# Loading batch 0 ahead, batch 1's transposes on TensorE, and pv per head with a column of ones

## The chip, the cores and the metric

The kernel runs on one core of a Trainium2 chip. The metric is the device time of one execution in microseconds (us). A profiled execution is read beside the timed ones; its times are us from the first instruction of the program. The engines are named as in the profile: PE is TensorE's matmuls and PEld its weight loads, DVE is VectorE, ACT is ScalarE, POOL is GpSimd, SP the queue that issues the DMAs.

## The reference

Sliding-window attention over 8 batches of 576 tokens with 8 heads of 64, and then a token mixer and an MLP on the result. Heads 0 to 3 see the last 32 tokens, heads 4 to 7 every fourth of the last 128.

```python
scores = scale * q @ k.T                      # (8, 8, 576, 576), scale 1/8
mask_plain = (rel >= 0) & (rel < 32)          # heads 0..3
mask_dil = (rel >= 0) & (rel < 128) & (rel % 4 == 0)   # heads 4..7
attn = exp(scores - max) ; attn /= sum(attn) + 1e-9
x = concat_heads(attn @ v)                    # (8, 576, 512), float32
h = x.T @ U @ V                               # U (576, 32), V (32, 576)
u = x + h.T
out = u + relu(u @ w_ch1) @ w_ch2             # 512 -> 2048 -> 512
```

The weights U, V, w_ch1 and w_ch2 reach the chip as 64-bit numbers and are turned into pairs of 32-bit numbers there.

## The kernel before, in words

**Attention.** The tokens of the dilated heads are reordered, so that both kinds of head have a band of 32. A batch has 9 blocks of 64 queries for each kind. A unit is one pair of heads and one block: its two heads lie in the 128 partitions of a tile (query of head 0, then of head 1), and its keys are 96. Four units are a group, 9 groups a batch (`NGB`). For a group, `score` multiplies queries and keys on TensorE (L392 in batches 0 and 1, L381 in most later groups, which are twice as wide and split into high and low parts first), `soften` masks and takes the negated maximum on DVE (L412) and the exponential on ACT (L416), whose accumulator gives the sum of the exponentials. `turn` transposes the result: on TensorE with a copy by DVE (L429, L433) for groups below `PE_T` = 12, that is batch 0 and three groups of batch 1, and otherwise with eight 32-row transposes on DVE (L442, L445). `weighted` multiplies by the values, four matmuls of 128 by 96 by 128, one for each unit (L453). One unit's product holds both heads' rows against both heads' values, of which only the two diagonal blocks are used. Each fp32 matmul appears as two instructions of TensorE. Then DVE adds 1e-9 to the sums (L454), takes the reciprocal (L455) and writes the products into the token tiles (L481); the dilated half goes through `xp` and DMAs (L485). A group's steps are spread over three turns of a loop (`LAG` = 2).

**Mixer and MLP.** For each batch, `split` makes high and low parts of x (L499, L501), `t_mm` multiplies by U (L521), `t_evict` and `mix` by V and add (L530 to L547). Token tiles are transposed (`transp`, L576 to L582, or `turn_x`) and go in chunks of three tiles through the MLP: 16 slices `f` of the hidden layer, for each 12 matmuls `ph` (L748), ReLU and split into `hh` on ACT and `hl` on DVE (L753, L754), and 9 matmuls `acc` (L765). The MLP is the bulk of TensorE's work. `weight_step` converts the weights piece by piece on ACT, DVE and POOL (L209 to L225).

**Order.** Batch 0's attention and mixer run first, then the MLP of the first chunk begins; the steps of batches 1 to 7 wait in a list, `queue`, with due times, and are put between the matmuls of the chunks. Weights are converted during batch 0, at a lower priority, and in the first chunk. A scheduler orders each engine's instructions at build time by priority and expected readiness. All loads go through SP.

**Loads of batches 0 and 1.** `load_qk` and `load_v` load a whole group, 448 KB of queries and keys and 192 KB of values. Five of the first and four of the second are issued ahead of all else (`FETCH` = 5); each turn of the loop issues those of a later group. Groups below `NE` = 7 take their queries and keys from such tiles, in four buffers (`QKS`); groups 7 and 8, and batch 1, fetch pairs of units (`fetch`, L339) into three buffers (`TB`). The pool `early` holds what batch 0 alone needs and is closed when it ends.

Of the kernel before, what the change touches and what calls it, by code (L numbers as in the profile page):

```python
# [10 lines left out]
F32 = mybir.dt.float32  # L11
F32R = mybir.dt.float32r
BF16 = mybir.dt.bfloat16
# [5 lines left out]
ALU = mybir.AluOpType  # L19

B, H, S, D = 8, 8, 576, 64
# [5 lines left out]
P = 128  # L27
QB = 64
NJ = S // QB
KB = QB + WIN  # L30
# [9 lines left out]
NCHUNK = NTILE // CT  # L40
UNITS = 4
QK1 = P + KB
KW = P + WIN
QK2 = P + KW
QK3 = P + 2 * KW
# [2 lines left out]
NGB = len(TILES) // 2  # L48
# [3 lines left out]
LAG = 2  # L52
# [7 lines left out]
H_ON_ACT = 3  # L60
XL_DVE = ((0, 1), (1, 1))
AHEAD = 2
FETCH = 5
POST_AT = 0.7
TAIL = 0.25
BLK = P // WIN
ZS = 2
NE = 7
QKB = 3
AHEAD_AT = 0.9  # L70
LO0 = 0.1
TB = 3
# [14 lines left out]
F_LAST = 13  # L87
RAWS = 4
VS = 4
QKS = 4  # L90
XPS = 4
VBS = 7
DVE_FROM = 2
TURN_AT = 0.5
TURN_GAP = 0.08
PT_ACT = ()
PE_T = 12
MASK_AT = (None, -16, 0, 16, 32, 48)
WIDE_AT = (None, 0, 16, 32, 48)
NEG = -8.0e9  # L100
# [50 lines left out]
def attention_moe_kernel(ctx: ExitStack, tc: tile.TileContext, qk1, qk2, vv, masks, wide, ident, ut, vt, w1, w2, out):  # L151
# [22 lines left out]
    HM = len(MASK_AT) // 2  # L174
    mask_sb = [work.tile([P, HM, KB], F32, tag="qk", name=f"mask{i}", bufs=QKB) for i in range(2)]
    spare = work.tile([P, QK2], F32, tag="qk", name="spare", bufs=QKB)
    wide_sb = const.tile([P, len(WIDE_AT), KW], BF16, name="wide_sb")
    id_sb = const.tile([P, P], F32, name="id_sb")
    us = const.tile([P, 9, 2 * RANK], F32R, name="us")
    vs = const.tile([P, P + S], F32R, name="vs")  # L180
# [117 lines left out]
    loaded = {}  # L298

    def load_qk(g):  # L300
        if g >= NE:
            if g == NE:
                for i in range(0, 2 * TB, 2):
                    fetch(UNITS * g + i)
        elif (g, 0) not in loaded:
            t = early.tile([P, UNITS, QK1], F32, tag="qk", name=f"qk{g}", bufs=QKS)
            nc.sync.dma_start(out=t, in_=qk1[g])
            loaded[g, 0] = t

    def load_v(g, i):  # L310
        if (g, 1, i) not in loaded:
            us_ = slice(2 * i, 2 * i + 2)
            if g < NGB:
                if i == 0:
                    t = early.tile([KB, UNITS, P], F32, tag="v", name=f"v{g}", bufs=VBS)
                    nc.sync.dma_start(out=t, in_=vv[g])
                    loaded[g, 1, 0] = t[:, 0:2]
                    loaded[g, 1, 1] = t[:, 2:4]
            else:
                t = work.tile([KB, 2, P], F32, tag="v", name=f"v{g}_{i}", bufs=3)  # L320
                nc.sync.dma_start(out=t, in_=vv[g][:, us_])
                loaded[g, 1, i] = t

# [44 lines left out]
    def score(g, u):  # L368
        n = UNITS * g + u
        two = n >= N2 and not is_odd(n)  # L370
        if u == 0:
            p_sb = work.tile([P, UNITS, KW], F32, tag="p", name=f"p{g}", bufs=2)
            pool, n_ = (early, 3) if g < NGB else (work, 2)
            nmax = pool.tile([P, UNITS], F32, tag="nmax", name=f"nmax{g}", bufs=n_)
            ssum = pool.tile([P, UNITS], F32, tag="ssum", name=f"ssum{g}", bufs=n_)
            state[g] = [p_sb, nmax, ssum, None]
        if two:
            sp = psum.tile([P, 2 * KW], F32, tag="ps", name=f"s{g}_{u}")
            split_qk(n)
            t = pairs.pop(n)  # L380
            nc.tensor.matmul(sp, lhsT=t[:, 0:P], rhs=t[:, P:], start=True, stop=True)  # L381
        else:
            if n >= N2:
                sp = psum.tile([P, 1, KB], F32, tag="ps", name=f"s{g}_{u}")
            elif u == 0:
                sp = psum.tile([P, UNITS, KB], F32, tag="acc" if g < NGB else "ps", name=f"s{g}", bufs=3)
            else:
                sp = state[g][3]
            if g >= NE:
                fetch(n)  # L390
            t = raws[n] if g >= NE else loaded[g, 0][:, u]
            nc.tensor.matmul(sp[:, u % sp.shape[1], :], lhsT=t[:, 0:P], rhs=t[:, P:QK1], start=True, stop=True)  # L392
        state[g][3] = state[g, u] = sp

    def soften(g, u):
        n = UNITS * g + u
        p_sb, nmax, ssum, _ = state[g]
        sp = state.pop((g, u))
        half, j = tile_of(g, u)
        every = slice(0, P)  # L400
        if n < N2:
            kind = mask_kind(half, j)
            todo = [(every, KB, sp[:, u], mask_sb[kind // HM][:, kind % HM])]
        elif is_odd(n):
            todo = [(slice(QB * h, QB * (h + 1)), KB, sp[QB * h:QB * (h + 1), 0],
                     wide_sb[QB * h:QB * (h + 1), 0, QB * h:QB * h + KB]) for h in range(2)]
        else:
            kind = mask_kind(half, tile_of(g, 0)[1] // 2, WIDE_AT, P)
            nc.vector.tensor_tensor(out=p_sb[:, u, :], in0=sp[:, 0:KW], in1=wide_sb[:, kind], op=ALU.add)  # L409
            todo = [(every, KW, sp[:, KW:], p_sb[:, u])]  # L410
        for rs, w, a, c in todo:
            nc.vector.tensor_tensor_reduce(  # L412
                out=p_sb[rs, u, 0:w], in0=a, in1=c, scale=-1.0 / 8.0, scalar=3.0e38,
                op0=ALU.add, op1=ALU.min, accum_out=nmax[rs, u:u + 1],
            )
        nc.scalar.activation(  # L416
            out=p_sb[:, u, 0:w], in_=p_sb[:, u, 0:w], func=AF.Exp,
            bias=nmax[:, u:u + 1], scale=-1.0, accum_out=ssum[:, u:u + 1],
        )

    def is_wide(g):
        return g >= SPLIT * NGB and g % NGB != ODD
# [22 lines left out]
                    nc.vector.transpose(out=pt[ks, :, rs], in_=p_sb[rs, :, ks])  # L445
        return pt

    def weighted(g, pt, ssum):
        b = g // NGB
        pv = psum.tile([P, UNITS, P], F32, tag="ps", name=f"pv{g}")  # L450
        for u in range(UNITS):
            v_sb = loaded[g, 1, u // 2]
            nc.tensor.matmul(pv[:, u, :], lhsT=pt[:, u, :], rhs=v_sb[:, u % 2, :], start=True, stop=True)  # L453
        nc.vector.tensor_scalar(out=ssum, in0=ssum, scalar1=1e-9, scalar2=None, op0=ALU.add)  # L454
        nc.vector.reciprocal(out=ssum, in_=ssum)  # L455
        moves = []
        xp = None
        for i in range(2):
# [18 lines left out]
            dst4 = dst.rearrange("p (u h d) -> p u h d", u=2, h=2)  # L477
            for h in range(2):
                rs = slice(QB * h, QB * (h + 1))
                norm = ssum[QB * i:QB * (i + 1), h::2] if is_wide(g) else ssum[rs, us_]  # L480
                nc.vector.tensor_tensor(  # L481
                    out=dst4[:, :, h, :], in0=pv[rs, us_, h * D:(h + 1) * D],
                    in1=norm.unsqueeze(2).broadcast_to([QB, 2, D]), op=ALU.mult)
        for t, to, n, r in sorted(moves):
            nc.sync.dma_start(out=x_tile(t)[to:to + DIL * (n - 1) + 1:DIL, HALF_D:], in_=xp[r:r + n])  # L485
        if moves and b == 0:
# [97 lines left out]
    def batch_items(b):  # L584
# [3 lines left out]
        for s in range(NGB + LAG):  # L588
            g = NGB * b + s

            def pre(s=s, g=g):
                if b == 0:
                    for i in (g, g + 1, g + FETCH):
                        if i < NGB:
                            load_qk(i)
                    if g + FETCH - 1 < NGB:
                        load_v(g + FETCH - 1, 0)
                if 0 < s <= NGB:
                    load_v(g - 1, 0)
                if s >= LAG:  # L600
                    weighted(g - LAG, *held.pop(g - LAG))
                if b > 0 and 0 < s <= NGB:
                    load_v(g - 1, 1)

            def post(s=s, g=g):
                late = g - (NGB * b < PE_T)
                if late in state and late not in turned:
                    turned.add(late)
                    p_sb, _, ssum, _ = state.pop(late)
                    held[late] = (turn(late, p_sb), ssum)  # L610

            def some(us, g=g):
                for u in us:
# [60 lines left out]
    early_open = ExitStack()  # L674
    early = early_open.enter_context(tc.tile_pool(name="early", bufs=1))
    held_u.append(early.tile([P, len(DPART), 2 * RANK], F32R, name="us_d"))
    for g in range(FETCH):
        load_qk(g)
        if g == 0:
            for i in range(2):  # L680
                nc.sync.dma_start(out=mask_sb[i], in_=masks[:, HM * i:HM * (i + 1)])
        if g == 1:
            nc.sync.dma_start(out=id_sb, in_=ident)
        if g < FETCH - 1:
            load_v(g, 0)
    pre = batch_items(0)
    w_prio = [tc.cur_priority + W_OFF]
    for i, (_, it) in enumerate(pre):
# [11 lines left out]
    for _ in range(PRE_N):  # L700
        weight_step(NSMALL, NPIECE)
    tc.cur_priority = now
    early_open.close()
    make_w(F_MID, F_LAST, None)

    def ahead(stage):
# [87 lines left out]
def lay_out(q, k, v, U, V, w1, w2):  # L794
# [1 line left out]
    f = np.float32  # L796
    qk1 = np.zeros((B, len(TILES), 2, P, QK1), f)
    qk2 = np.zeros((B - SPLIT, NGB, UNITS, P, QK2), f)
    vv = np.zeros((B, len(TILES), 2, KB, P), f)
    for half in range(2):  # L800
        perm = np.array([token_of(half, s) for s in range(S)])
        hs = slice(half * HH, (half + 1) * HH)
# [5 lines left out]
        for j in range(NJ):  # L808
            at = TILES.index((half, j))
            ks = slice(QB * j, QB * j + KB)  # L810
            for h in range(2):
                hr = slice(h * D, (h + 1) * D)
                qk1[:, at, :, hr, h * QB:(h + 1) * QB] = qp[:, :, h, QB * j:QB * (j + 1)].transpose(0, 1, 3, 2)
                qk1[:, at, :, hr, P:] = kp[:, :, h, ks].transpose(0, 1, 3, 2)
                vv[:, at, :, :, hr] = vp[:, :, h, ks]
        for i in range(NJ // 2):
            g = TILES.index((half, 2 * i)) // 2
            for u in range(UNITS):
# [4 lines left out]
    qk2[:, ODD, :, :, :QK1] = qk1[SPLIT:, ODD]  # L823
    qk2 = qk2.reshape((B - SPLIT) * NGB * UNITS, P, QK2)
    qk1 = np.ascontiguousarray(qk1[:SPLIT].reshape(SPLIT * NGB, UNITS, P, QK1).transpose(0, 2, 1, 3))
    vv = np.ascontiguousarray(vv.reshape(B * NGB, UNITS, KB, P).transpose(0, 2, 1, 3))

    masks = np.stack([np.tile(mask_of(off, QB), (2, 1)) for off in MASK_AT], axis=1)
    wide = np.stack([mask_of(off, P) for off in WIDE_AT], axis=1).astype(ml_dtypes.bfloat16)
# [41 lines left out]
```

## Time and profile before

| | |
|---|---|
| median of 3 runs | 1032.8 us (1031.57 to 1034.27) |
| profiled execution | 1032.92 us, span 1031.1 us |
| mean granted TensorE clock | 0.974 |
| PE, busy | 992.3 us (96%) |
| PEld, busy | 894.4 us (87%) |
| DVE, busy | 643.8 us (62%) |
| ACT, busy | 436.8 us (42%) |
| POOL, busy | 323.4 us (31%) |
| bytes moved | 103.05 MB |

The page of the profile gives each engine's busy time, the span in 40 slices of 25.8 us with the busy tenths of each, the chain of work that ended last, and groups of equal instructions with their count, busy time and mean length. The matmuls of TensorE overlap in their pipeline, so a matmul's own length is more than what it holds up; what it holds up is read from one start to the next.

### The profile page before, as it was taken

The page shows a single profiled execution, that of the slowest core. Times are in us where ns is not written, and L with a number is a line of the kernel's source. Part 1 is how long each engine was busy: PE and PEld are TensorE (multiplying, and loading weights), DVE is VectorE, ACT ScalarE, POOL GpSimd, SP SyncE. Part 2 cuts the span into 40 slices and gives each one's busy share as a digit, 9 for nine tenths or more (in the row PEclk, how much of TensorE's full clock was granted, in tenths as well). Part 3 has the DMA queues.
Part 4 walks back from the last instruction along what each step waited for, and adds up shares of the span by engine and source line. Part 5 has one row for each costly group of instructions (what it writes and reads, how often), then busy time and mean ns, then how long its engine had stood idle before and what let it go on. Part 6 is the DMA issues. An engine that isn't in the chain of part 4 may idle for free.

```text
span 1031.1 us, 17355 instructions
## 1 busy us (share of the span) xinstructions
PE 992.3 (96%) x5304; PEld 894.4 (87%) x5304; DVE 643.8 (62%) x2197; ACT 436.8 (42%) x1274; POOL 323.4 (31%) x519
## 2 busy tenths in 40 slices
PE   6769998999999999999999999999999999999998
PEld 5658887998899899998899898999889898999996
DVE  5888987877457863877557864777647874311211
ACT  5888874454244432444233532544324442111110
POOL 1476644353132630434122621335213431000000
PEclk9658999999999999999999999999999999999999
DMA  9767544243232433333232432424223321400000
GB/s 281 215 197 231 173 142 118 78 128 87 78 98 71 123 84 78 108 104 99 72 96 80 128 82 61 131 82 126 85 73 86 119 65 30 125 1 1 31 1 31
DMA packets 97197, 103.05 MB, mean 100 GB/s; under 512 B 12848, under 2 KB 84080, under 8 KB 97104
## 3 DMA queue, kind: packets, MB, share of 16 engines
q1 hardware_dynamic: 97104, 101.94, 34.6%
q8 instruction: 43, 0.70, 0.3%
q14 instruction: 50, 0.41, 0.1%
HBM read 79.86 MB, written 17.30 MB: 94 GB/s over the span
## 4 chain that ended last, share of the span: by engine, by line
PE 82%; DVE 10%; DMA 4%; ACT 3%; issue 1%; SPq 0%; POOL 0%; DVEq 0%; POOLq 0%; ACTq 0%
PE ph L748 36%; PE acc L765 35%; PE pv L453 5%; PE s L381 3%; PE t L521 2%; DVE pt L445 2%; DMA qk<-qk 1%; PE s L392 1%; DVE utl L582 1%; DMA qkr<-qk 1%; DMA v<-vv 1%; DVE v L217 1%; PE m L545 1%; ACT p L416 1%; DVE xp L481 1%
## 5 line engine op out<-in xcount | busy, mean ns | idle before, releaser
L765 PE MATMUL acc<-w2h,hh 128*128 128x512 f32 x576 | 229.4, 398 | 0.0
L765 PE MATMUL acc<-w2l,hh 128*128 128x512 f32 x576 | 228.5, 397 | 0.0
L357 POOL TENSOR_TENSOR qks<-qkr,qks 128x160 fp32r<-128x160 f32 x192 | 104.5, 544 | 376.8 <-ACT qks L356 254.4
L765 PE MATMUL acc<-w2h,hl 128*128 128x512 f32 x576 | 213.4, 397 | 1.6 <-DVE hl L754 1.6
L753 ACT ACTIVATE hh<-ph 128x384 fp32r<-128x384 f32 x192 | 93.6, 487 | 284.4 <-PE ph L748 274.6
L754 DVE SCALAR_TENSOR_TENSOR hl<-ph,hh 128x384 fp32r<-128x384 f32 x192 | 106.0, 552 | 167.5 <-ACT hh L753 167.0
L416 ACT ACTIVATE p<-p,nmax 128x160 f32<-128x160 f32 (+1 forms) x288 | 117.2, 408 | 137.4 <-DVE nmax L412 135.3
L748 PE MATMUL ph<-uth,w1h 128*128 128x384 f32 x768 | 175.3, 342 | 0.0
L748 PE MATMUL ph<-uth,w1l 128*128 128x384 f32 x768 | 174.6, 340 | 0.0
L748 PE MATMUL ph<-utl,w1h 128*128 128x384 f32 x768 | 173.3, 339 | 0.0
L748 PEld LDWEIGHTS ph<-uth,w1h 128*128 128x128 f32 x768 | 139.5, 190 | 15.0 <-ACT uth L581 0.3
L748 PEld LDWEIGHTS ph<-uth,w1l 128*128 128x128 f32 x768 | 136.8, 189 | 0.5
L748 PEld LDWEIGHTS ph<-utl,w1h 128*128 128x128 f32 x768 | 135.8, 188 | 1.5
L765 PEld LDWEIGHTS acc<-w2h,hl 128*128 128x128 f32 x576 | 108.1, 189 | 24.4 <-DVE hl L754 2.5
L442 DVE STREAM_TRANSPOSE pt<-p 32x128 f32<-32x128 f32 x384 | 115.9, 302 | 19.7 <-ACT p L416 14.5
L765 PEld LDWEIGHTS acc<-w2h,hh 128*128 128x128 f32 x576 | 109.2, 190 | 15.6 <-ACT hh L753 0.2
L765 PEld LDWEIGHTS acc<-w2l,hh 128*128 128x128 f32 x576 | 109.1, 189 | 14.8
L356 ACT CAST qks<-qkr 128x288 fp32r<-128x288 f32 x192 | 81.7, 430 | 84.7 <-PE s L381 58.7
L360 POOL TENSOR_TENSOR qks<-qkr,qks 64x128 fp32r<-64x128 f32 x192 | 90.1, 470 | 15.1
L409 DVE TENSOR_TENSOR p<-s,wide_sb 128x160 f32<-128x160 f32 x192 | 60.6, 319 | 46.6 <-PE s L381 44.6
L453 PE MATMUL pv<-v,pt 96*128 96x128 f32 x576 | 80.1, 283 | 3.8 <-DVE pt L445 1.7
L453 PEld LDWEIGHTS pv<-v,pt 96*128 96x128 f32 x576 | 77.2, 199 | 7.1 <-DVE pt L433 2.0
(68 smaller groups left out, 1052.9 us busy)
## 6 DMA issues: line engine op xcount, KB each, us to landing
qkr<-qk SPq DMA_DIRECT2D x192, 144.0 KB, 2.2
raw<-w SPq DMA_DIRECT2D x26, 512.0 KB, 5.1
v<-vv SPq DMA_DIRECT2D x126, 96.0 KB, 2.1
out<-x SPq DMA_DIRECT2D x36, 256.0 KB, 2.3
zd<-z SPq DMA_DIRECT2D x120, 64.0 KB, 1.9
xt<-zd SPq DMA_DIRECT2D x30, 256.0 KB, 2.8
qkr<-qk SPq DMA_DIRECT2D x22, 224.0 KB, 3.4
qk<-qk SPq DMA_DIRECT2D x7, 448.0 KB, 7.7
```

The lines of the kernel that those rows point to most:

```text
L356: nc.scalar.copy(out=t[:, 0:QK2], in_=raw)
L357: nc.gpsimd.tensor_tensor(out=t[:, QK2:], in0=raw[:, P:], in1=t[:, P:QK2].bitcast(F32), op=ALU.subtract)
L360: eng.tensor_tensor(out=t[lo, 0:P], in0=raw[lo, 0:P], in1=t[lo, 0:P].bitcast(F32), op=ALU.subtract)
L381: nc.tensor.matmul(sp, lhsT=t[:, 0:P], rhs=t[:, P:], start=True, stop=True)
L409: nc.vector.tensor_tensor(out=p_sb[:, u, :], in0=sp[:, 0:KW], in1=wide_sb[:, kind], op=ALU.add)
L416: nc.scalar.activation(out=p_sb[:, u, 0:w], in_=p_sb[:, u, 0:w], func=AF.Exp, bias=nmax[:, u:u + 1], scale=-1.0, accum_out=ssum[:, u:u + 1],)
L442: nc.vector.transpose(out=to[:, :, WIN * (r % 2):WIN * (r % 2 + 1)], in_=p_sb[rs, :, QB * s + WIN * k:QB * s + WIN * (k + 1)])
L453: nc.tensor.matmul(pv[:, u, :], lhsT=pt[:, u, :], rhs=v_sb[:, u % 2, :], start=True, stop=True)
L748: nc.tensor.matmul(ph, lhsT=w[:, k, :], rhs=u[:, k, :], start=(n == 0), stop=(n == len(seq) - 1))
L753: nc.scalar.activation(out=hh, in_=ph, func=AF.Relu)
L754: nc.vector.scalar_tensor_tensor(out=hl, in0=ph, scalar=0.0, in1=hh.bitcast(F32), op0=ALU.max, op1=ALU.subtract)
L765: nc.tensor.matmul(acc[i], lhsT=h[:, ss], rhs=w, start=(f == 0 and n == 0), stop=(f == FC - 1 and n == 2))
```

## The change

Three things are changed together.

1. All nine groups of batch 0 are loaded whole, each into its own buffer (`NE` and `QKS` are 9), and all these loads are issued at the start, the second half of the masks after the third group. The values go into slots of the pool of the x tiles. The first three fetches of batch 1 stand behind batch 0's steps. The wide masks get a place in a pool that opens when `early` closes.
2. `PE_T` becomes 18: groups 12 to 17, the last six of batch 1, are transposed on TensorE.
3. `weighted` multiplies each head by itself: eight matmuls for a group, with 64 columns of the transposed exponentials as weights and 65 columns of values, the last of which is one. Head 0's product goes to partitions 0 to 63 and head 1's to 64 to 127. The 65th column is the sum, which DVE reads from PSUM; the exponential on ACT has no accumulator any more. The loaded values have 65 columns for each head.

```diff
+DV = D + 1
+PV = 2 * DV
-FETCH = 5
-NE = 7
+NE = 9
-QKS = 4
+QKS = 9
-VBS = 7
-PE_T = 12
+PE_T = 18
...
     def load_qk(g):
-        if g >= NE:
-            if g == NE:
-                for i in range(0, 2 * TB, 2):
-                    fetch(UNITS * g + i)
-        elif (g, 0) not in loaded:
+        if (g, 0) not in loaded:
             t = early.tile([P, UNITS, QK1], F32, tag="qk", name=f"qk{g}", bufs=QKS)
...
-                    t = early.tile([KB, UNITS, P], F32, tag="v", name=f"v{g}", bufs=VBS)
+                    t = xpool.tile([P, UNITS, PV], F32, tag="x", name=f"v{g}")[0:KB]
...
-                t = work.tile([KB, 2, P], F32, tag="v", name=f"v{g}_{i}", bufs=3)
+                t = work.tile([KB, 2, PV], F32, tag="v", name=f"v{g}_{i}", bufs=3)
...
         nc.scalar.activation(
             out=p_sb[:, u, 0:w], in_=p_sb[:, u, 0:w], func=AF.Exp,
-            bias=nmax[:, u:u + 1], scale=-1.0, accum_out=ssum[:, u:u + 1],
+            bias=nmax[:, u:u + 1], scale=-1.0,
         )
...
-    def weighted(g, pt, ssum):
+    def weighted(g, pt):
         b = g // NGB
-        pv = psum.tile([P, UNITS, P], F32, tag="ps", name=f"pv{g}")
+        pv = psum.tile([P, UNITS, DV], F32, tag="ps", name=f"pv{g}")
         for u in range(UNITS):
             v_sb = loaded[g, 1, u // 2]
-            nc.tensor.matmul(pv[:, u, :], lhsT=pt[:, u, :], rhs=v_sb[:, u % 2, :], start=True, stop=True)
-        nc.vector.tensor_scalar(out=ssum, in0=ssum, scalar1=1e-9, scalar2=None, op0=ALU.add)
+            for h in range(2):
+                hs = slice(h * DV, (h + 1) * DV)
+                nc.tensor.matmul(pv[QB * h:QB * (h + 1), u, :], lhsT=pt[:, u, QB * h:QB * (h + 1)],
+                                 rhs=v_sb[:, u % 2, hs], start=True, stop=True)
+        pool, n_ = (early, 3) if g < NGB else (work, 2)
+        ssum = pool.tile([P, UNITS], F32, tag="ssum", name=f"ssum{g}", bufs=n_)
+        nc.vector.tensor_scalar(out=ssum, in0=pv[:, :, D], scalar1=1e-9, scalar2=None, op0=ALU.add)
         nc.vector.reciprocal(out=ssum, in_=ssum)
...
-                norm = ssum[QB * i:QB * (i + 1), h::2] if is_wide(g) else ssum[rs, us_]
                 nc.vector.tensor_tensor(
-                    out=dst4[:, :, h, :], in0=pv[rs, us_, h * D:(h + 1) * D],
-                    in1=norm.unsqueeze(2).broadcast_to([QB, 2, D]), op=ALU.mult)
+                    out=dst4[:, :, h, :], in0=pv[rs, us_, 0:D],
+                    in1=ssum[rs, us_].unsqueeze(2).broadcast_to([QB, 2, D]), op=ALU.mult)
...
             def pre(s=s, g=g):
-                if b == 0:
-                    for i in (g, g + 1, g + FETCH):
-                        if i < NGB:
-                            load_qk(i)
-                    if g + FETCH - 1 < NGB:
-                        load_v(g + FETCH - 1, 0)
...
-    for g in range(FETCH):
+    for g in range(NGB):
         load_qk(g)
         if g == 0:
-            for i in range(2):
-                nc.sync.dma_start(out=mask_sb[i], in_=masks[:, HM * i:HM * (i + 1)])
-        if g == 1:
+            nc.sync.dma_start(out=mask_sb[0], in_=masks[:, 0:HM])
             nc.sync.dma_start(out=id_sb, in_=ident)
-        if g < FETCH - 1:
-            load_v(g, 0)
+        if g == 2:
+            nc.sync.dma_start(out=mask_sb[1], in_=masks[:, HM:])
+        load_v(g, 0)
...
+    for i in range(0, 2 * TB, 2):
+        fetch(UNITS * NGB + i)
     early_open.close()
+    rest = ctx.enter_context(tc.tile_pool(name="rest", bufs=1))
+    wide_sb = rest.tile([P, len(WIDE_AT), KW], BF16, name="wide_sb")
     make_w(F_MID, F_LAST, None)
...
-    vv = np.zeros((B, len(TILES), 2, KB, P), f)
+    vv = np.ones((B, len(TILES), 2, KB, PV), f)
...
-                vv[:, at, :, :, hr] = vp[:, :, h, ks]
+                vv[:, at, :, :, h * DV:h * DV + D] = vp[:, :, h, ks]
```

More of the change, by code (lines that the diff above doesn't have):

```diff
@@ L176, in attention_moe_kernel @@
     spare = work.tile([P, QK2], F32, tag="qk", name="spare", bufs=QKB)
-    wide_sb = const.tile([P, len(WIDE_AT), KW], BF16, name="wide_sb")
     id_sb = const.tile([P, P], F32, name="id_sb")
@@ L374, in score @@
             nmax = pool.tile([P, UNITS], F32, tag="nmax", name=f"nmax{g}", bufs=n_)
-            ssum = pool.tile([P, UNITS], F32, tag="ssum", name=f"ssum{g}", bufs=n_)
-            state[g] = [p_sb, nmax, ssum, None]
+            state[g] = [p_sb, nmax, None]
         if two:
@@ L387, in score @@
             else:
-                sp = state[g][3]
+                sp = state[g][2]
             if g >= NE:
@@ L392, in score @@
             nc.tensor.matmul(sp[:, u % sp.shape[1], :], lhsT=t[:, 0:P], rhs=t[:, P:QK1], start=True, stop=True)
-        state[g][3] = state[g, u] = sp
+        state[g][2] = state[g, u] = sp
     def soften(g, u):
         n = UNITS * g + u
-        p_sb, nmax, ssum, _ = state[g]
+        p_sb, nmax, _ = state[g]
         sp = state.pop((g, u))
@@ L600, in pre @@
                 if s >= LAG:
-                    weighted(g - LAG, *held.pop(g - LAG))
+                    weighted(g - LAG, held.pop(g - LAG))
                 if b > 0 and 0 < s <= NGB:
@@ L608, in post @@
                     turned.add(late)
-                    p_sb, _, ssum, _ = state.pop(late)
-                    held[late] = (turn(late, p_sb), ssum)
+                    held[late] = turn(late, state.pop(late)[0])
             def some(us, g=g):
@@ L825, in lay_out @@
     qk1 = np.ascontiguousarray(qk1[:SPLIT].reshape(SPLIT * NGB, UNITS, P, QK1).transpose(0, 2, 1, 3))
-    vv = np.ascontiguousarray(vv.reshape(B * NGB, UNITS, KB, P).transpose(0, 2, 1, 3))
+    vv = np.ascontiguousarray(vv.reshape(B * NGB, UNITS, KB, PV).transpose(0, 2, 1, 3))
     masks = np.stack([np.tile(mask_of(off, QB), (2, 1)) for off in MASK_AT], axis=1)
```

## The prediction

> **What bounds the kernel now.** I read the page first: the engines' shares, the 40 slices and the chain.
>
> ```profile
> span 1031.1 us, 17355 instructions
> PE 992.3 (96%) x5304; PEld 894.4 (87%) x5304; DVE 643.8 (62%) x2197; ACT 436.8 (42%) x1274; POOL 323.4 (31%) x519
> PE   6769998999999999999999999999999999999998
> DVE  5888987877457863877557864777647874311211
> ACT  5888874454244432444233532544324442111110
> PEclk9658999999999999999999999999999999999999
> PE 82%; DVE 10%; DMA 4%; ACT 3%; issue 1%; SPq 0%; POOL 0%; DVEq 0%; POOLq 0%; ACTq 0%
> ```
>
> TensorE is full from the seventh slice on. Only the first six, some 155 us, are not all its own: there DVE and ACT mostly stand at 8, and the granted clock falls to 0.5 in one slice. So two prices are wanted: what the change does to TensorE's own time, which is paid in full after about 180 us, and what it does to the stretch before. The windows put sizes to it.
>
> ```profile
> 0.00:26.00 26.00, 16.59 (x101) 14.84 (x101) 13.69 (x80) 13.33 (x54) 3.26 (x8) 0.98 0.97 281
> 26.00:70.00 44.00, 29.85 (x124) 24.00 (x125) 39.79 (x99) 36.48 (x90) 26.36 (x23) 0.58 0.68 210
> 70.00:180.00 110.00, 101.48 (x552) 89.81 (x551) 89.30 (x274) 83.21 (x225) 64.92 (x61) 0.94 0.55 167
> 180.00:1031.00 851.00, 844.39 (x4532) 765.72 (x4530) 501.05 (x1747) 303.82 (x908) 228.81 (x428) 1.00 0.29 80
> ```
>
> The columns are TensorE, its weight loads, DVE, ACT, POOL, granted clock, DMA share and GB/s. Up to 26 us the DMA is the limit (0.97 of the time) and DVE has 12.3 us idle. From 26 to 70 DVE works 39.8 of 44 us and ACT 36.5. After 180 us no engine but TensorE is near its limit. The profiled execution took 1032.9 us in all, 1.8 more than its span and 0.1 more than the median of the three runs; the sum is made against it. About 0.3% (3.1 us) is what a measurement of this kernel can tell from no change.
>
> **The loads first.** Batch 0 needs nine query/key and nine value tiles. Today seven of the query/key tiles come through four buffers, and the last two groups in pairs through three others. These rows, of the timeline and of the groups, show what that makes late and what DVE spends on a group.
>
> ```profile
> 27.79 2.77 PE L392 MATMUL s<-qkr 128*128 128x96 f32 x12
> ...
> 36.86 0.69 PE L392 MATMUL s<-qkr 128*128 128x96 f32 x4
> ...
> 28.88 2.03 SPq L339 DMA_DIRECT2D qkr<-qk  x3
> ...
> 49.49 1.22 DVE L481 TENSOR_TENSOR xp<-pv,ssum 64x128 f32<-64x128 f32 x4
> ```
>
> ```profile
> L412 DVE CUSTOM_DVE_ANT_0 p<-s,mask 128x96 f32<-128x96 f32 x72 | 14.3, 252 | 12.2 <-PE s L392 12.0
> L433 DVE COPY pt<-ptp 96x512 f32<-96x512 f32 x12 | 8.2, 682 | 3.0 <-PE ptp L429 2.7
> ```
>
> The pair for the last scores of batch 0 is issued at 28.9 us, the scores run at 36.9, and the last weighting on DVE ends at 50.7. After the change the queue holds 9 x 448 KB, 9 x 195 KB, the masks and the identity, 6.1 MB, ahead of anything else; at the 281 GB/s of the first window that has landed by about 24 us. A group costs DVE four softmax steps (0.2 each), a copy (0.69), four weightings (1.22) and two small operations on the sums: some 3 us, 27 for nine. If DVE starts at 6 us and works four fifths of the time, 16 of these are done by 26; with 7 us that I allow for splits and small weights the rest ends at about 44 instead of 50.7. Against these 6 to 7 us stands that U, V and the MoE weights now queue on SP behind six more loads, and ACT has to convert them.
>
> ```profile
> 19.06 0.62 ACT L209 ACTIVATE v<-raw 128x448 f32<-128x448 f32 x1 [0.75 <-DMA raw<-ut]
> ...
> 32.50 0.68 ACT L209 ACTIVATE v<-raw 128x512 f32<-128x512 f32 x1 [2.15 <-DMA raw<-w]
> ```
>
> The first of these moves from 19 to some 25 us, and with it about 4.5 us of ACT work into the stretch where ACT is short. The second stands behind 7.8 MB, 28 us at that rate, so it need not be later than its 32.5. I take -6 us. The ends are -12, all of DVE's idle time in the first window, and +3, ACT's 4.5 us with little gained elsewhere. Batch 1's first pairs, today the other two issues of the row at 28.9 us, are written behind batch 0's steps and are wanted only once the MoE runs. The wide masks, loaded after batch 0's pool closes, are read from batch 2 on; batch 1 covers both, and without that cover TensorE would stand for a load's time, once. The value tiles take nine slots of the x pool beside batch 0's five, of 16, so none waits.
>
> **The sums.** ACT loses a read of its accumulator.
>
> ```profile
> L416 ACT ACTIVATION_READ_ACCUMULATOR p<-p,nmax 128x1 f32 x288 | 54.4, 189 | 0.0
> ...
> 23.06 0.35 ACT L416 ACTIVATE p<-p,nmax 128x96 f32<-128x96 f32 x1
> 23.32 0.19 ACT L416 ACTIVATION_READ_ACCUMULATOR p<-p,nmax 128x1 f32 x1
> 23.41 0.36 ACT L416 ACTIVATE p<-p,nmax 128x96 f32<-128x96 f32 x1
> ```
>
> Start to start a step takes 0.35 us; without the read the next could start at 23.32, 0.09 earlier. That is 26 us over 288 steps: worth nothing after 180 us, where ACT works 304 of 851 us, and 3.2 us in each of the first two batches. The first 3.2 are spent against the 4.5 above; for batch 1 I take -1.5 (ends 0 and -3.2). On DVE the small sum (L454) now reads PSUM and has to follow the matmul. The weightings behind it waited for the same matmul already, so what is queued behind them on DVE, the `hl` that TensorE needs in the MoE, is held by the two small operations at most, 0.35 us a group; DVE's idle third after 180 us covers it, and without that cover 54 groups would pay 19 us.
>
> **Batch 1's transposes.** Between 69 and 180 us DVE's groups have these rows:
>
> ```profile
> L445 DVE STREAM_TRANSPOSE pt<-p 32x128 f32<-32x128 f32 x48 | 14.5, 301 | 1.7 <-ACT p L416 1.1
> ...
> L454 DVE TENSOR_SCALAR ssum<-ssum 128x4 f32<-128x4 f32 x9 | 6.2, 690 | 0.2
> ```
>
> and TensorE's timeline these:
>
> ```profile
> 110.39 1.05 PE L453 MATMUL pv<-v,pt 96*128 96x128 f32 x8
> 111.28 1.03 PE L392 MATMUL s<-qkr 128*128 128x96 f32 x8
> ...
> 118.92 1.16 PE L453 MATMUL pv<-v,pt 96*128 96x128 f32 x8 [1.71 <-DVE pt L445]
> ...
> 121.79 0.63 PE L765 MATMUL acc<-w2h,hl 128*128 128x512 f32 x1
> 122.22 0.63 PE L765 MATMUL acc<-w2h,hh 128*128 128x512 f32 x1
> ```
>
> The 48 transposes are the six groups that move, 14.5 us, against six copies, 4.1: DVE gets 10 back. TensorE takes on 24 instructions of 128 columns; at the 111 ns that the eight of `pv` take each (0.89 us to the next start) that is +2.6, and since TensorE works 92% of this stretch I charge all of it. It buys off one stall, 1.7 us, and behind it eight matmuls at the slow clock, 0.43 us apart where 0.23 is usual: 3.3 in all. Net -0.7; the ends are +2.6, the stall merely changing its cause, and -6, if the other waits of the stretch shrink too. ACT, 83 of 110 us busy, is late next. L454's 690 ns for four numbers a row is mostly not work; whether a PSUM source avoids it no row shows, and as it is DVE's time I count none of its 4 us.
>
> **The weighting per head, on TensorE.** Instead of eight instructions there are sixteen, each with 64 instead of 128 weight columns and 65 instead of 128 moving ones.
>
> ```profile
> L453 PEld LDWEIGHTS pv<-v,pt x416: 187/192/193, 201.0 to 855.6; 96*128 96x128 f32 x139
> L453 PE MATMUL pv<-v,pt x416: 272/275/302, 201.2 to 855.7; 96*128 96x128 f32 x139
> ...
> L392 PE MATMUL s<-qkr x16: 243/259/275, 203.8 to 330.6; 128*128 128x96 f32 x16
> ...
> L521 PEld LDWEIGHTS t<-xhl,us x60: 129/134/136, 359.7 to 627.4; 128*64 128x64 f32 x48, 64*64 64x64 f32 x12
> ```
>
> (Shortest, median and longest duration in ns.) A load of 64 columns is 58 ns shorter than one of 128, so half a load is 56 of the 111. A scores matmul that its weights do not hold is 243 against 275: 32 ns for 32 columns. Down from 111 that gives 48 for 65 columns, in proportion 56. Both streams fall to half, sixteen take 0.90 us, and the next full load shows 55 ns that a longer matmul would have covered: 0.95, less 0.89, is +0.06 a group. 61 groups pay, 54 of batches 2 to 7 and some 7 of batch 1: +3.5 us. No row has a matmul that writes partitions 64 to 127. The ends: below, the two halves beside each other, 8 x 56 + 55 = 0.50 us, -24; above, a price at either side of the group as the one other small shape pays it, +24.
>
> ```profile
> 385.20 0.33 PE L521 MATMUL t<-xhl,us 64*64 64x256 f32 x1
> 385.45 0.50 PE L765 MATMUL acc<-w2h,hh 128*128 128x512 f32 x1
> 385.79 0.39 PE L765 MATMUL acc<-w2l,hh 128*128 128x512 f32 x1
> 386.02 0.39 PE L765 MATMUL acc<-w2h,hl 128*128 128x512 f32 x1
> ...
> 387.30 0.40 PE L521 MATMUL t<-xhl,us 128*64 128x256 f32 x2
> 387.53 0.34 PE L748 MATMUL ph<-uth,w1h 128*128 128x384 f32 x1
> ```
>
> The 64*64 step holds the next for 0.25 us and that one for 0.34, where a 512-column matmul takes 0.23 and a step of the 128*64 shape half of 0.23; with its own late start the detour is about 0.34. The 128*64 pair, whose shape the new matmuls have, costs no more than its columns. I take +3.5 as that row is the nearest. The Trainium skill, TensorEngine Tiling (Array Packing), Key Properties, says that changing the tiling mode drains TensorE; by that rule this term would be +24. The 64*64 rows agree with it, the 128*64 rows do not.
>
> **Sum.** 1032.9 - 6 - 1.5 - 0.7 + 3.5 = 1028.2.
>
> **The rivals.** (1) The halves overlap: they use different columns of the array and need nothing of each other. If loads and streams both run beside each other, the last term is -24 and the time 1001. For it speaks that the weight loads, 87% of the span, hide behind matmuls already; against it, that every row has them one after the other, and sixteen loads of 56 ns in a row leave nothing to gain. The same Key Properties let different tiles load and multiply in parallel. (2) Slower: the shape change costs each group the 0.34 us of the 64*64 step, 61 x 0.34 = 21 more, 1049. It decides from 0.08 us a group upward, where the other terms' 4.7 us of gain are gone. Against it is the 128*64 row; for it, that no row has the second half's place. (3) The early loads change nothing: ACT's conversions, in 36.5 busy of 44 us, set when the MoE goes on, the -6 becomes 0, and the time is 1034.2.
>
> **How the numbers follow.** The forecast is the sum's case, 0.36, with its own range 1020 to 1034; rival 3 has 0.13, 1031 to 1038; rival 1 0.31, 994 to 1010; rival 2 0.20, 1038 to 1056. Faster than 1029.7: rival 1 and 0.25 of the first case, 0.56. Within 0.3%: 0.09 of the first, 0.08 of rival 3 and 0.01 of rival 2, 0.18. Slower: the rest, 0.26. From 997 to 1051 a tenth is left out at either end.
>
> **What would show it.** Right: sixteen `pv` matmuls in 0.9 to 1.0 us in the steady stretch; 0.27 us between ACT's softmax steps; no L445 before 160 us; batch 0's last scores before 30 us, and the first `ph` some 6 us earlier than today. Wrong: the sixteen in under 0.7 us (rival 1) or over 1.2 (rival 2); a first `ph` that comes early and then waits for weights (rival 3); `hl` held behind the small sums.

## The result, and the profile after

| | before | after |
|---|---|---|
| median of 5 runs, us | 1033.7 (1031.6 to 1034.3) | 1024.3 (1021.9 to 1024.8) |
| profiled execution, us | 1032.9 | 1021.9 |
| span, us | 1031.1 | 1020.1 |

The ratio is 0.9911, with a 95% interval of 0.9896 to 0.9926: about 9 us faster, where 1028.2 was forecast, some 5 us faster. One of the runs below, of e4, took 1101.4 us at a granted clock of 0.84 and is left out of its row. The page of the changed kernel, its engines, TensorE's slices and granted clock, and the chain:

```profile
span 1020.1 us, 18204 instructions
PE 982.4 (96%) x5904; PEld 861.3 (84%) x5904; DVE 625.1 (61%) x2155; ACT 411.2 (40%) x986; POOL 324.2 (32%) x519
PE   7479998999999999999999999999999999999998
PEclk9579997999999999999999999999999999999999
PE 87%; DMA 5%; DVE 3%; ACT 2%; SPq 1%; issue 1%; POOL 0%; DVEq 0%; ACTq 0%; POOLq 0%
```

The same shape as before: TensorE full but for the first slices. The windows of the changed kernel, in the columns of the ones before:

```profile
0.00:26.00 26.00, 19.55 (x196) 17.57 (x196) 14.77 (x90) 9.93 (x30) 1.20 (x6) 1.00 0.96 298
26.00:70.00 44.00, 24.89 (x130) 18.16 (x128) 38.70 (x92) 36.31 (x77) 27.39 (x24) 0.61 0.61 193
70.00:180.00 110.00, 103.95 (x672) 89.43 (x671) 80.03 (x257) 82.38 (x193) 71.01 (x70) 0.95 0.59 179
```

TensorE and DVE do more in the first window and ACT less (9.9 us for 13.3), since U comes later and the reads of its accumulator are gone. TensorE's timeline of the changed kernel has batch 0's last scores and the first `ph`; ACT's has a group's four softmax steps and the first conversion of U:

```profile
24.71 0.36 PE L386 MATMUL s<-qk 128*128 128x96 f32 x2
...
63.88 1.65 PE L742 MATMUL ph<-uth,w1h 128*128 128x384 f32 x4
```

```profile
21.95 1.17 ACT L410 ACTIVATE p<-p,nmax 128x96 f32<-128x96 f32 x4 [0.38 <-DVE nmax L406]
25.55 0.61 ACT L208 ACTIVATE v<-raw 128x448 f32<-128x448 f32 x1 [2.43 <-DMA raw<-ut]
```

The scores end at 25 instead of 37 us, the first `ph` starts at 63.9 instead of 69.5, four steps in 1.17 us are 0.27 us apart, and U is converted from 25.6 on: each as the prediction has it.

A group's `pv` matmuls stand between whole-width ones; call that a visit. How long it holds TensorE is read from the starts around it. First the kernel before, then the changed one, both in the steady stretch:

```profile
431.69 0.31 PE L381 MATMUL s<-qks 128*128 128x320 f32 x1
431.83 1.05 PE L453 MATMUL pv<-v,pt 96*128 96x128 f32 x8
432.64 0.48 PE L765 MATMUL acc<-w2h,hl 128*128 128x512 f32 x1
432.95 0.40 PE L765 MATMUL acc<-w2h,hh 128*128 128x512 f32 x1
```

```profile
415.93 0.40 PE L759 MATMUL acc<-w2h,hh 128*128 128x512 f32 x1
416.26 0.69 PE L449 MATMUL pv<-v,pt 96*64 96x65 f32 x16
416.87 0.42 PE L375 MATMUL s<-qks 128*128 128x320 f32 x1
417.13 0.39 PE L759 MATMUL acc<-w2l,hh 128*128 128x512 f32 x1
```

One `s` (0.15 us) and one `acc` (0.23) stand beside the visit each time. Before: 432.95 - 431.69 - 0.38 = 0.88 us. After: 417.13 - 415.93 - 0.38 = 0.82. The sixteen themselves take 0.61 from first start to next start, but the first starts 0.10 us later behind its `acc` than an `acc` would, and the `s` after them holds 0.26 instead of 0.15. In the records of the single instructions the first `pv` ends 201 ns after the `acc` (111 for the whole-width one), the others end 6 and 52 ns apart by turns, two in 58 ns, and what follows ends 0.20 us late. So the halves seem to run beside each other (0.46 us for sixteen instead of 0.9), and going in and out costs 0.34: 0.14 that the first takes over its 58 ns, and these 0.20.

### The profile page after: what moved, and what is told of

Read it like the earlier page. It is cut to its first block, busy times and chain, and to the rows that moved or that the text cites. A ratio compares the mean times of both kernels' runs of the same rounds, so it can differ in the third digit from the quotient of the medians.

```text
span 1020.1 us, 18204 instructions
## 1 busy us (share of the span) xinstructions
PE 982.4 (96%) x5904; PEld 861.3 (84%) x5904; DVE 625.1 (61%) x2155; ACT 411.2 (40%) x986; POOL 324.2 (32%) x519
## 4 chain that ended last, share of the span: by engine, by line
PE 87%; DMA 5%; DVE 3%; ACT 2%; SPq 1%; issue 1%; POOL 0%; DVEq 0%; ACTq 0%; POOLq 0%
PE ph L742 38%; PE acc L759 38%; PE pv L449 4%; PE s L375 3%; PE t L519 2%; PE s L386 1%; DMA zd<-z 1%; DMA raw<-ut 1%; PE m L543 1%; DMA qk<-qk 1%; SPq L483 1%; DMA x<-xp 1%; DMA qkr<-qk 1%; DMA v<-vv 1%; DMA raw<-w 0%
## 5 line engine op out<-in xcount | busy, mean ns | idle before, releaser
L759 PE MATMUL acc<-w2h,hl 128*128 128x512 f32 x576 | 210.9, 398 | 0.0
L410 ACT ACTIVATE p<-p,nmax 128x160 f32<-128x160 f32 (+1 forms) x288 | 111.4, 410 | 122.7 <-DVE nmax L406 119.2
L499 POOL TENSOR_TENSOR xhl<-x,xhl 128x256 fp32r<-128x256 f32 (+1 forms) x70 | 51.6, 759 | 87.7 <-ACT xhl L497 55.1
L406 DVE CUSTOM_DVE_ANT_0 p<-s,p 128x160 f32<-128x160 f32 x192 | 60.3, 320 | 3.7
## 6 DMA issues: line engine op xcount, KB each, us to landing
out<-x SPq DMA_DIRECT2D x36, 256.0 KB, 2.2
xt<-zd SPq DMA_DIRECT2D x30, 256.0 KB, 2.8
```

Source lines behind the costliest of these rows:

```text
L406: nc.vector.tensor_tensor_reduce(out=p_sb[rs, u, 0:w], in0=a, in1=c, scale=-1.0 / 8.0, scalar=3.0e38, op0=ALU.add, op1=ALU.min, accum_out= ...
L410: nc.scalar.activation(out=p_sb[:, u, 0:w], in_=p_sb[:, u, 0:w], func=AF.Exp, bias=nmax[:, u:u + 1], scale=-1.0,)
L499: eng.tensor_tensor(out=xl[rs], in0=x[rs], in1=xh[rs].bitcast(F32), op=ALU.subtract)
L759: nc.tensor.matmul(acc[i], lhsT=h[:, ss], rhs=w, start=(f == 0 and n == 0), stop=(f == FC - 1 and n == 2))
```

## The experiments

The first `ph` below is the MLP's first matmul; the MoE of the prediction is the MLP. The theory: part three was mis-sized, since both halves' overlap and the price of the shape are real and nearly cancel, and the other terms are as forecast. The rival: part three costs what was forecast, and the surplus comes out of the first 180 us. Of each profiled execution the table has the first `ph`, and the first sum of `acc` and x on DVE of the second and of the last chunk (the chunk rate between them is TensorE's). A profile is one execution: the changed kernel and e10, which compute batch 0 alike, have their first `ph` 1.3 us apart, so differences of that size in the table tell nothing.

| kernel | median, us | ratio to before, 95% | first `ph` | 2nd chunk | last chunk |
|---|---|---|---|---|---|
| before | 1032 to 1034 | 1 | 69.5 | 261.4 | 1025.6 |
| changed (all three parts) | 1024.3 | 0.9911 (0.9896 to 0.9926) | 63.9 | 254.5 | 1015.1 |
| e1: loads | 1026.3 | 0.9948 (0.9929 to 0.9966) | 63.1 | 255.8 | 1019.3 |
| e2: transposes | 1031.6 | 0.9993 (0.9980 to 1.0005) | 70.3 | 261.4 | 1025.6 |
| e3: pv per head and sums | 1021.0 | 0.9890 (0.9872 to 0.9909) | 62.4 | 251.2 | 1013.3 |
| e4: loads and transposes | 1026.5 | 0.9947 (0.9930 to 0.9965) | 61.9 | 255.2 | 1018.7 |
| e5: pv per head, sums from ACT | 1029.7 | 0.9964 (0.9951 to 0.9977) | 66.4 | 255.1 | 1019.1 |
| e6: e3, two groups a visit | 1034.9 | 1.0024 (1.0011 to 1.0037) | 62.3 | 253.0 | 1026.9 |
| e7: changed, U sooner | 1026.6 | 0.9946 (0.9919 to 0.9972) | 66.4 | 255.6 | 1015.8 |
| e9: e3, 128 rows | 1020.2 | 0.9885 (0.9864 to 0.9906) | 62.4 | 251.5 | 1013.2 |
| e10: changed, 128 rows | 1024.7 | 0.9928 (0.9911 to 0.9946) | 65.2 | 256.0 | 1017.0 |
| e11: e3 and transposes | 1023.2 | 0.9918 (0.9900 to 0.9937) | 63.5 | 256.2 | 1016.4 |

**The parts apart (e1 to e4).**

```diff
 e1: NE = 9, QKS = 9, all of batch 0's loads first, as in the change; nothing else
 e2: PE_T = 18; nothing else
 e3: weighted, its sums and the values' layout as in the change; loads and PE_T as before
 e4: e1 and e2 together
```

> The kernel before with only the loads of batch 0 put first. Theory A (pv per head is what the forecast mis-sized: head halves overlap in pairs, and the shape change costs 0.34 us a group; the loads are worth what was forecast): first ph at 64 us, total 1027 to 1029 (-5 to -7). Rival B (pv per head costs about the +3.5 us of the forecast, and the surplus of 5 us comes out of the first 180 us): total below 1025.

> The kernel before with only PE_T = 18. Theory A: net -0.7 us as forecast, 1031 to 1035, first ph unchanged at 69.5 us. Rival B: the transposes shorten the stretch from 70 to 180 us by more than the forecast, 1027 to 1030.

> The kernel before with only pv per head and the sums from the column of ones. Theory A: a group of pv holds TensorE 0.81 us against 0.89, 60 groups x -0.08 = -5 us, and ACT's reads give another 1 to 2: 1027 to 1030. Rival B: 1035 to 1038 (+3.5 with little from ACT).

> The changed kernel without its third part: loads first and PE_T = 18, but pv whole and the sums from ACT's accumulator. Theory A: 5 to 6 us slower than the changed kernel, 1029 to 1031; after 254 us it loses those by 0.08 us a group. Rival B: faster than the changed kernel or equal to it, 1020 to 1024.

e1 and e2 came out as the theory said: -5.4 us, and -0.7, which is not told apart from nothing. e4 lies between the two, below the theory's 1029 and above the rival's 1024: by the ratios part three on top of it brings 3.7 us, where the theory had 5 to 6. e3 missed by most: alone it brings 11 us, where both theories had it between -6 and +5. Its trace has most of that ahead of the steady stretch: the first `ph` is 7 us earlier, and the second chunk 10, without any early load. So the parts don't add: -5.4 and -11.4 alone, about -9 together with the transposes. That e1 and e3 buy the same wait is likely and not shown.

**The two halves of part three (e5).** Against e3, the sums come from ACT's accumulator again, and DVE's small operation reads them from SBUF; the column of ones is multiplied and not used.

```diff
-            bias=nmax[:, u:u + 1], scale=-1.0,
+            bias=nmax[:, u:u + 1], scale=-1.0, accum_out=ssum[:, u:u + 1],
```

> The kernel with only pv per head, but the sums still come from ACT's accumulator (the column of ones is multiplied and not used). If ACT's 36 reads in batch 0 (6.8 us busy) are what brought the first ph from 69.5 to 62.4 us with part three alone: first ph back at 68 to 70, total 1027 to 1030, and after 260 us the same pace as part three alone. If it was pv per head: first ph 62 to 64, total 1020 to 1023.

TensorE's timelines of e5 and of e3, where the mixer ends:

```profile
66.01 0.58 PE L550 MATMUL m<-ts,vs 128*128 128x256 f32 x1 [2.21 <-DVE x L552]
66.39 0.84 PE L753 MATMUL ph<-uth,w1h 128*128 128x384 f32 x2
```

```profile
62.13 0.39 PE L550 MATMUL m<-ts,vs 128*128 128x256 f32 x1 [0.51 <-DVE x L552]
62.36 0.86 PE L752 MATMUL ph<-uth,w1h 128*128 128x384 f32 x4
```

The first `ph` falls back by 4 of the 7 us, not to 68, and the time by 0.74% of 1033, about 7.6 us (its runs lie between 1026 and 1032). So by the totals the sums are the larger half of part three, pv per head the smaller, 3.7 us. ACT's 36 reads in front of the first `ph` (6.8 us) come off the engine that the mixer's `xhl` and `ts` and the conversions wait for. DVE's small sum gets shorter too: 18.7 us for 72 of them before, in the changed kernel

```profile
L453 DVE TENSOR_SCALAR ssum<-pv 128x4 f32<-128x4 f32 x72 | 11.4, 159 | 9.1 <-PE pv L449 8.2
```

which answers what the prediction left open: with a PSUM source the 690 ns for four numbers are gone. Between 69 and 180 us the mean is 435 ns in e5, from SBUF, and 156 in e3, from PSUM. How the 7.6 us divide between the reads and this was not tried.

e5's steady stretch, with the cheaper visits, is as long as before's (764 us between the two chunks of the table; e3 762, changed kernel 760.5). The traces show where the gain goes. A slice of the last chunk, where no attention is left, before and in e5:

```profile
973.70 0.86 PE L748 MATMUL ph<-uth,w1h 128*128 128x384 f32 x4
975.80 0.40 PE L765 MATMUL acc<-w2h,hh 128*128 128x512 f32 x1
977.86 0.86 PE L748 MATMUL ph<-uth,w1h 128*128 128x384 f32 x4
```

```profile
975.41 0.86 PE L753 MATMUL ph<-uth,w1h 128*128 128x384 f32 x4
977.49 0.39 PE L770 MATMUL acc<-w2h,hh 128*128 128x512 f32 x1
979.59 0.86 PE L753 MATMUL ph<-uth,w1h 128*128 128x384 f32 x4
```

Twelve `ph` take 2.08 instead of 2.10 us and nine `acc` 2.10 instead of 2.06, at a granted clock of 1.00 in both. The last two chunks last 66.7 and 63.0 us before and in e2, and 67.1 to 67.2 and 63.3 to 63.5 in e3, e5 and the changed kernel: some 0.4 us a chunk, 4 us over ten if all lengthen alike, about what 54 cheaper visits save. Why the MLP's own matmuls lengthen with part three is open. So the 6 us that e5's profiled execution gains (its fastest, 1026.3 us) stand ahead of the second chunk, and its total does not confirm the price of the visits.

**Where the 0.34 us comes from (e6, e8, e9, e10, e12).** Of the visits of other shapes (rows by weight columns; fp32r is the type in which the mixer's `t` is multiplied), 96 x 128 fp32 and 128 x 64 fp32r pay nothing, 64 x 64 fp32r pays. Each of these kernels changes one thing, e12 two that are read apart.

```diff
 e8, on the changed kernel: both heads into the lower half
-                nc.tensor.matmul(pv[QB * h:QB * (h + 1), u, :], ...
+                nc.tensor.matmul(pv[0:QB, u, :], ...
 e6, on e3: from batch 2 on, two groups' pv back to back (3 buffers for pt, 5 for v)
-                if s >= LAG:
-                    weighted(g - LAG, held.pop(g - LAG))
+                if s >= LAG and (b < SPLIT or (s - LAG) % 2 or s == NGB + LAG - 1):
+                    for i in (g - LAG - 1, g - LAG):
+                        if i in held:
+                            weighted(i, held.pop(i))
 e9, on e3 (e10, on the changed kernel): pt and v padded to 128 rows, batches 1 to 7
+        ks = slice(0, KB if b == 0 else P)
-                ... lhsT=pt[:, u, ...], rhs=v_sb[:, u % 2, hs]
+                ... lhsT=pt[ks, u, ...], rhs=v_sb[ks, u % 2, hs]
 e12, on e3: t as fp32; in odd groups h outside, u inside
-                t_ps[b, c], lhsT=u[rs], rhs=m[rs],
+                t_ps[b, c], lhsT=u[rs].bitcast(F32), rhs=m[rs].bitcast(F32),
```

> The changed kernel with both heads' products written to partitions 0 to 63, one over the other, so that all sixteen loads and matmuls take the same half of the array's columns; the second head's result stands for both. If the pairs of 6 and 52 ns in the trace are two matmuls running beside each other in the two halves of the columns: sixteen ends 58 ns apart, 0.93 us a group instead of 0.46. If the 0.34 us round the group comes from leaving column 0, it goes; if it comes from the shape of 96 rows by 64 columns, it stays. Total +28 us with the price left, +8 us without it, near 1052 and 1032; if the halves aren't what overlaps, 1024.

One run, 1048.9 us, nearest the case in which the price is left. A visit in TensorE's timeline:

```profile
434.86 0.40 PE L759 MATMUL acc<-w2l,hh 128*128 128x512 f32 x1
435.18 1.15 PE L449 MATMUL pv<-v,pt 96*64 96x65 f32 x16
436.26 0.50 PE L759 MATMUL acc<-w2h,hl 128*128 128x512 f32 x1
436.60 0.86 PE L742 MATMUL ph<-uth,w1h 128*128 128x384 f32 x4
```

436.60 - 434.86 - 2 x 0.23 = 1.28 us, and the sixteen end 58 ns apart: on one half of the columns they follow each other, as the forecast had it, and the 0.34 stays. So the overlap is that of the two halves, and the price isn't that of leaving column 0. (Both heads' products also go to the same place of PSUM here; the odd groups of e12, below, set that aside.)

> Part three alone, and from batch 2 on the pv of two groups stand back to back (five visits a batch instead of nine; a third buffer for the transposed exponentials, five for the values). If a visit costs TensorE 0.34 us for the change of shape whatever its length: 6 x 4 = 24 visits less, -8 us, about 1013, and a double visit holds TensorE 0.34 + 2 x 0.46 = 1.27 us. If the price is one of each matmul: no change, 1019 to 1023. If the doubled pv makes DVE or the buffers late: above 1023.

```profile
428.55 0.86 PE L754 MATMUL ph<-uth,w1h 128*128 128x384 f32 x4
429.34 1.15 PE L456 MATMUL pv<-v,pt 96*64 96x65 f32 x32
430.42 0.42 PE L382 MATMUL s<-qks 128*128 128x320 f32 x1
430.68 0.69 PE L754 MATMUL ph<-uth,w1l 128*128 128x384 f32 x3
```

430.68 - 428.55 less four `ph` (0.70) and an `s` (0.15) is 1.28 us for 32: one price for a double visit, as expected. The time went the other way all the same. The waits of e6's TensorE after 180 us begin with

```profile
PE ph L754 <- ACT uth L586: 10.8, 3, 3.8
```

Three chunks start 3.6 us late on average, for the transposed x. The first of these waits ends at 409 us; the granted clock is 0.50 from 409 to 413 us, and its mean is 0.74 from 404 to 417, 0.86 round the second wait (644 to 656) and 0.83 round the third (880 to 900), which makes up to 8 us more. The first group of each pair gets its weighting a turn later, which is the likely reason and was not tried by itself. Waits and slow clock, up to 19 us, eat the 8 us and most of the 14 by which the kernel ends behind e3.

> Part three alone, with the pv of batches 1 to 7 over 128 rows instead of 96: the transposed exponentials have zeros in rows 96 to 127, and the values come padded to 128 rows (4.2 MB more are loaded). The 0.34 us round a visit was paid by 96 rows x 64 columns and by 64 x 64, not by 128 x 64 nor by 96 x 128. If it takes a shape short in rows and in columns: it goes, a visit holds TensorE 0.46 to 0.5 us instead of 0.81, 61 visits x 0.34 = 20 us, total 1000 to 1004. If it belongs to the fp32 form or to the walk between the halves: no change, 1020 to 1024.

```profile
413.36 0.40 PE L770 MATMUL acc<-w2h,hh 128*128 128x512 f32 x1
413.69 0.69 PE L457 MATMUL pv<-v,pt 128*64 128x65 f32 x16
414.30 0.42 PE L382 MATMUL s<-qks 128*128 128x320 f32 x1
414.56 0.39 PE L770 MATMUL acc<-w2l,hh 128*128 128x512 f32 x1
```

> The changed kernel with the same padding. If the price goes: 20 us less than the changed kernel, 1002 to 1006; if not, 1023 to 1026.

With all 128 rows a visit holds 414.56 - 413.36 - 0.38 = 0.82 us as with 96, and neither kernel moved. The rows don't matter; a miss of my idea, and the 4.2 MB cost nothing here.

> Part three alone with two edits that are read in the trace, not in the total. First, the mixer's t is multiplied as fp32 instead of as fp32r, with the same 128 rows by 64 columns at column 0. As fp32r it enters with 0.116 us, its own columns, and leaves with nothing on top. If the 0.34 us of the pv visits belongs to fp32 with 64 columns: t now enters with some 0.14 us over its own length and what follows ends 0.2 us late. If it belongs to something else in pv: t only gets longer. Second, in odd groups all eight matmuls of head 0 stand in front of the eight of head 1. If two matmuls overlap only when neighbours take different halves of the columns: ends 58 ns apart in the odd groups, with one step of 6 at the border, and 6 and 52 in the even ones. If the queue reorders them: 6 and 52 in both. Total 1021 to 1050, the longer t in it.

One run, 1082.7 us, 33 us over the upper end expected: `t` is twice as many instructions, 320 for 160, each with nearly twice the step (216 ns for 116). The mixer's `t` as fp32, and a visit of `pv` in an odd group:

```profile
525.56 0.86 PE L754 MATMUL ph<-utl,w1h 128*128 128x384 f32 x4
526.34 0.65 PE L528 MATMUL t<-xhl,us 128*64 128x256 f32 x2
526.92 0.50 PE L771 MATMUL acc<-w2h,hh 128*128 128x512 f32 x1
527.25 0.39 PE L771 MATMUL acc<-w2l,hh 128*128 128x512 f32 x1
...
451.53 0.97 PE L458 MATMUL pv<-v,pt 96*64 96x65 f32 x16
```

Two `t` of 216 ns each (end to end in a run of them) hold TensorE for 527.25 - 525.56 - 0.70 - 0.23 = 0.76 us: 0.33 more than their columns. The first ends 361 ns after the `ph`, 145 over its own, and the `acc` behind ends 0.2 late; as fp32r the same 128 x 64 shape came in with 116 ns and left with nothing. So fp32 with 64 columns pays the price also outside `pv`. A `pv` that follows such a `t` ends 59 ns behind it: between two of that kind there is none. In the odd groups five end 58 ns apart, then three pairs 2 or 3 ns apart, then five alone again, so that sixteen take 0.90 to the next start instead of 0.61. By strict order only one of each head could overlap, at the border; so TensorE seems to start a matmul of the other half past a few that wait, which I had not expected. The order by turns is better.

**Which of the first two parts costs the changed kernel its lead (e7, e11).** e3 has 0.9890, all three parts 0.9911.

```diff
 e7, on the changed kernel, in the loop of the loads:
+        if g == 4:
+            for n in range(2):
+                sent.setdefault(0, []).append(n)
+                pipe[n] = fetch64(n)
```

> The changed kernel, with the loads of U and of the first half of V put behind the fifth group's loads instead of behind the ninth's. If the early loads bring nothing beside part three because U lands at 25.5 us instead of 18.0 and ACT's conversions pile up behind it: U lands near 15 to 18, ACT's idle time before them goes, first ph at 60 to 62 instead of 63.9, total 1020 to 1022. If not (DVE's or POOL's work sets it): first ph 63 to 65, total 1023 to 1025.

```profile
16.99 0.60 ACT L208 ACTIVATE v<-raw 128x448 f32<-128x448 f32 x1 [3.01 <-DMA raw<-ut]
...
66.40 1.65 PE L746 MATMUL ph<-uth,w1h 128*128 128x384 f32 x4
```

U lands at 17.0 us, and the first `ph` comes later, not sooner. It and the total (1026.6 us, with runs from 1022.6 to 1030.9) lie above both cases expected. U's place in the queue isn't the cause; that the loads of the last four groups now stand behind those of U and V may cost something of its own.

> Parts two and three without the early loads, to find which of the first two costs the changed kernel its 3 us against part three alone. If the early loads do (they bring nothing more in front of the first ph, and ACT's conversions and POOL's come later): 1020 to 1022. If the transposes on TensorE do (24 more instructions there, 2.6 us): 1023 to 1025.

e11 has 0.9918, close to the changed kernel's 0.9911: the transposes cost some 3 us beside part three, and the early loads then bring nothing that can be told. In the trace the second chunk ends at 256.2 against 251.2 in e3, but not for the instructions themselves. From the first `ph` to the first chunk's sum, where all 24 of them run, e3 takes 96.2 us and e11 96.1; from there to the second chunk's sum, where there are none, 92.7 and 96.5. Without part three it is 103.0 and 88.9 before, 97.8 and 93.3 in e2: a gain in the first chunk and a loss in the second. TensorE in the 20 us behind the first chunk, in e3 and in e11:

```profile
160.00:180.00 20.00, 17.60 (x91) 15.46 (x92) 17.20 (x64) 10.19 (x25) 9.06 (x19) 0.83 0.57 153
```

```profile
160.00:180.00 20.00, 15.67 (x77) 13.18 (x76) 16.12 (x55) 9.16 (x22) 7.85 (x16) 0.74 0.50 142
```

In e11 it works 1.9 us less there, at a granted clock of 0.74 against 0.83. Why the second chunk's start suffers is open. The intervals of e3 and e11 overlap a little; e3 and the changed kernel with padding, e9 and e10, stand as far apart (0.9885 and 0.9928). Part three alone, with either number of rows, is the best of these kernels, by some 3 us.

## Why the prediction came out as it did

The forecast's direction and its range hold; of its four terms two hold by themselves, and two don't stand as they were put. That the time lies in the range is in part luck, as the end of this section shows.

**pv per head: +3.5 forecast, -4 to -5 by the visits, -3.7 by the total.** The failed step is "both streams fall to half, sixteen take 0.90 us", and behind it the choice of the 128 x 64 row as the nearest. The halves overlap (rival 1's mechanism; sixteen loads of 56 ns in a row would not fit into 0.46 us, so the loads overlap too) and the shape costs 0.34 us a visit (rival 2's), both near the size given for them: 0.46 + 0.34 is 0.80, and 0.82 by the starts, against 0.88, so 61 x -0.06 to -0.08 is -4 to -5 us. That the total of e5 says the same is luck: the visits' gain in the steady stretch goes into the longer matmuls of the MLP, and e5's stands ahead of it. Each rival was taken to exclude the other, and their sum was none of the cases. The 128 x 64 row misled since it is fp32r; the row named for rival 2, 64 x 64, had the right price. The Trainium skill, TensorEngine Tiling (Array Packing), Key Properties, has both halves of the answer, different tiles in parallel and a drain on a change of mode; these runs agree with both for fp32 (58 ns for a pair, 0.34 us a visit). That 128 x 64 in fp32r pays no drain fits what the Trainium skill, PSUM — Partial Sum Buffer, The four PSUM rules, mentions by the way: float32r matmuls force the mask of all column groups, so such a one would not change the tiling of the columns. The runs show only the missing price, not the mask. The sign "under 0.7 us, rival 1" was badly chosen too: sixteen in 0.61 are there, and rival 1's 24 us are not, as the time lies in the first's late end and in what follows.

**The sums: -1.5 forecast, about -7.6 alone.** The reads were sized right (0.27 us a step, so 26 us in all), but batch 0's 3.2 us were written off against the conversions, and the chain of ACT, DVE and POOL before the first `ph` was taken to be set by the loads. e3 and e5 show that ACT's reads, the small sum or both stand on that chain (first `ph` at 62.4 and 66.4 us); which of the two is not shown.

**The loads: -6 forecast, -5.4 alone, nothing that can be told beside part three.** The step was right by itself; adding it to the sums was wrong. Rival 3 is what happened in the company of part three, but ACT's conversions as its reason find no support: in e7 they began early and nothing was gained. What sets the first `ph` there is not settled.

**Batch 1's transposes: -0.7 forecast, -0.7 alone (not told apart from nothing), some +3 beside part three.** The upper end, +2.6, is near what came, but not by its mechanism. In e3 no stall of `pv` on its transposes is among TensorE's waits, so there was none to buy off; yet the 24 instructions cost nothing that the first chunk shows, and the loss stands in the second. No transpose of L445 (L439 now) comes before 205 us, as forecast.

So the sum of -4.7 stands for about -9.2. Added in this order, the ratios give -3.7 for pv per head, -7.6 for the sums, +2.9 for the transposes and -0.7 for the loads, each with some 2 us of uncertainty; another order would divide them otherwise. The first two came out 13 us below their forecasts and the last two 9 above: these misses nearly cancel, which is luck. `hl` was not held behind the small sums: after 260 us TensorE waits 1.1 us for DVE's sum of `acc` and x and 0.3 for the transposed x, and for nothing else.

## What to carry to other kernels

Before two mechanisms are set against each other as rivals, ask whether both can hold at once, and give their sum a case. Gains of two changes need not add: price each part with the others already in place, and run the parts alone, since here one of three beats all three. Put two half-width fp32 matmuls side by side by turns, keep the visits to that shape few, but look at who waits for the last of a longer visit.

## What the runs showed of the hardware

- Two fp32 matmuls of 64 weight and 65 moving columns take 58 ns as a pair on different halves of the array (changed kernel); on the same half they take 58 ns each (e8).
- fp32 with 64 columns between whole-width matmuls costs 0.34 us a visit, some 0.14 going in and 0.20 coming out, with 96 and 128 rows and with 16, 32 or 2 instructions (changed kernel, e9, e6, e12); 128 x 64 in fp32r costs nothing, 64 x 64 in fp32r does (before).
- A tiny DVE operation of 128 x 4 takes 159 ns from PSUM on average (changed kernel), where from SBUF it took 260 and, between 69 and 180 us, 690 (before).
